# A three-stage attention and expert kernel: the hand-out of Strassen inputs and of the first pair's GpSimd sums, moved to later steps

## The chip, the cores and the metric

The kernel runs on one core of a Trainium2 chip. The metric is the device time of one execution in microseconds (us). Engines are named as the profile names them: PE (TensorE matmul; PEld its weight load), DVE (VectorE), ACT (ScalarE), POOL (GpSimd) and SP (SyncE, which here only issues DMAs).

## What is computed

Three stages follow each other (cut from the reference):

```
attn_out = attention(q, k, v)          # 4 x 8 heads, 576 positions, two masks
x = attn_out as 2304 tokens x 512
h = x @ w_in;  x = (h - tanh(h)) @ w_out              # 512 -> 2048 -> 512
xn = x / sqrt(mean(x*x) + 1e-6) * rms_g
y = (silu(xn @ w_gate) * (xn @ w_val)) @ w_out2       # 512 -> 1536 -> 512
```

## The kernel before

Every fp32 product is made of three matmuls on a high and a low half (`hi*hi + hi*lo + lo*hi`), so each operand needs a cast (high) and a subtraction (low) before PE can use it.

The attention and the first expert run until about 466 us. The second expert works on the first 256 tokens plainly and on the other 2048 by one level of Strassen's scheme (seven products in place of eight). The **plain part** is the loop over `f` at lines 1388 to 1399, 12 steps (`FB` = 12), one for each 128 columns of `w_gate` and `w_val`. A step prepares weights ahead (`st2.to`: load `raw`, ACT splits the bits at L184 and L186, DVE merges them into `ct` at L196, ACT casts the high half at L203, DVE subtracts the low half at L207), stores the merged weights to DRAM (`v`, L344, from ACT's queue) and the split ones (`w`, L363, from SP's), and issues the step's matmuls (`pe_gv`, into `ps_h`), then those of the step two before into the output sums (`pe_o`, into `ps_x`). `pe_gv` also issues the step's activation: SiLU (L949), product (L950), high and low half `p` (L952, L953).

Two generators are drawn from in the same loop:

- `pg` is `preps()`. When the loop begins seven items are left: `conv(m)` for m = 1, 2, 5, 6, 3, 7, 4. Each makes one Strassen input `xt` for tokens 256 to 1279: a subtraction `tr` (L1039, for m = 5, 6, 7 and 4), a cast (L1058, ACT) and a subtraction (L1059, DVE) on 128x1024 tiles.
- `decode.to(n)` runs the first n of a list. For the first **pair** (two 128-column blocks of the weights) these are eight: load the four stored tiles `v` into two `wa` tiles (L291), four sums or differences `ws` on POOL (L302) and the high and low halves `wo` of the results (L285, L286), for gate and then for val; one of the eight is empty. The tiles `tr`, `wa` and `ws` share a pool of four buffers.

After the loop comes `Stage.run` for the first pair: product 1 (`ps_pr` from `wt`), the last plain `pe_o`, then product 5 (`ps_pr` from `wo`), product 2 (`ps_q`), and 6, 3, 7, 4. Product 5 multiplies by the first `wo` of gate and then of val.

The order on the engines is made when the program is built: a scheduler with a model of its own sorts ACT, DVE and POOL by the place in the program and by priorities (`tc.high_priority`), while SP and, after the loop, PE keep the order of the program. A tile is written only when a buffer of its pool is free. DMAs of SP and ACT share eight completion counters in turn, and each DMA waits until the one that used its counter before has landed.

Of the kernel before, what the change touches and what calls it, by code (L numbers as in the profile page):

```python
# [34 lines left out]
def attn_moe_moe_kernel(  # L35
# [25 lines left out]
    B, _, NC, D = q_str.shape  # L61
    NT, DM = out.shape
    FA = w_in.shape[0]
    FB = w_gate.shape[0]
# [16 lines left out]
    def runs(s):  # L81

        r = []
        for i, (b, t) in enumerate(subs[s]):
            if r and r[-1][0] == b and r[-1][1] + r[-1][2] == t:
                r[-1][2] += 64
            else:
                r.append([b, t, 64, 64 * i])
        return r
# [36 lines left out]
    for s in range(len(subs)):  # L126
        if len(runs(s)) > 1 or s in LANES:
            _, t0, n, _ = runs(s)[0]
# [201 lines left out]
    decode = Decode()  # L330
# [606 lines left out]
    def pe_gv(j, f):  # L937
        r, n = [], R0
        bank = (bank_h, bank_m, bank_h, bank_m, bank_x, bank_x)[f % 6]("ps_h")
        for k, kd in enumerate(("gate", "val")):  # L940
            ps = bank[:, k * n:k * n + n]
            w, x = w2[kd, f].t, xn[j]
            seq = [(a, e, c) for c in range(4) for a, e in ((0, 0), (0, 1), (1, 0))]
            for i, (a, e, c) in enumerate(seq):
                mm(ps, w[:, a, c, :], x[:, e, c, :], i == 0, i == len(seq) - 1)
            r.append(ps)
        with tc.high_priority(400):
            s = pb.tile([128, n], F32, tag="s", name="s", bufs=3)
            nc.scalar.activation(out=s, in_=r[0], func=ACTF.Silu, scale=WS)  # L949
            nc.vector.scalar_tensor_tensor(out=s, in0=r[1], scalar=WS, in1=s, op0=ALU.mult, op1=ALU.mult)  # L950
            t = pb.tile([128, 2, n], F32R, tag="p", name="p", bufs=3)
            nc.scalar.copy(out=t[:, 0], in_=s)  # L952
            nc.vector.tensor_tensor(out=t[:, 1], in0=s, in1=t[:, 0].bitcast(F32), op=ALU.subtract)  # L953
        p_of[j, f] = t

    def pe_o(j, f):
        if f == 0:
            oacc[j] = [ps_x.tile([128, 512], F32, tag="x", name="ps_x") for _ in range(R0 // 128)]
        w, p = w2["out2", f].t.rearrange("p s c f -> p s (c f)"), p_of.pop((j, f))
        for t in range(R0 // 128):  # L960
            for i, (a, e) in enumerate(((0, 0), (1, 0), (0, 1))):
                mm(
                    oacc[j][t], p[:, e, t * 128:t * 128 + 128], w[:, a, :],
                    f == 0 and i == 0, f == FB - 1 and i == 2,
                )
# [422 lines left out]
    for f in range(FB):  # L1388
        if f == FB - 4:
            pairs[0].fetch((0, 1))  # L1390
        st2.to(max(3 * (f + 2), N1 + (len(w2_order) - N1) * (f + 1) // (FB - 2)))
        store.plain(st2.i - 1)
        store.to(st2.i - 6)
        pe_gv(0, f)
        for _ in range(3 if f < FB - 2 else 40):
            next(pg, None)
        decode.to(max(0, min(8, 8 * (f - 4) // 6)))
        if f > 1:
            pe_o(0, f - 2)
    pe_o(0, FB - 2)  # L1400
# [154 lines left out]
```

## Time and profile before

| | us |
|---|---|
| median of 3 runs | 888.45 |
| lowest, highest run | 885.4, 888.65 |
| profiled execution, its own time | 887.88 |
| its span | 886.1 |
| PE busy in the span | 866.5 |
| DVE, ACT, POOL busy | 629.8, 413.9, 250.6 |

The span is counted from the first instruction; about 1.8 us of the execution's own time lie outside it. In a timeline a row merges instructions of one kind that follow each other: start, duration, engine, line, tiles, count, and in brackets how long the engine stood idle before and what released it. `SPq` and `ACTq` rows are the queues at which DMAs are issued. The table by stretch gives for each engine the busy us and the number of instructions, then the clock granted to PE as a share of full speed, the busy share of the DMA engines and the rate.

### The profile page before, as it was taken

To read this page: it belongs to the slowest core of one execution; us is meant where nothing else is said; L and a number is where in the kernel's file an instruction comes from. 1 tells how busy PE (TensorE), PEld (TensorE's weight loads), DVE (VectorE), ACT (ScalarE), POOL (GpSimd) and SP (SyncE) were. 2 spreads that over 40 slices of the span, in tenths; PEclk is the share of its full clock that TensorE was granted. 3 is DMA by queue.
4 is the path that set the end of the run, shared out by engine and by line. 5 is a ranking of instruction groups with operands and counts; after the bars stand their busy time and mean duration, and the time that the engine had idled before them with its cause. 6 is when DMAs were issued, how large, how long until landed. Compare 5 with 4: busy or idle time off the path is not lost.

```text
span 886.1 us, 14047 instructions
## 1 busy us (share of the span) xinstructions
PE 866.5 (98%) x5091; PEld 722.7 (82%) x5091; DVE 629.8 (71%) x1290; ACT 413.9 (47%) x916; POOL 250.6 (28%) x309
## 2 busy tenths in 40 slices
PE   7999999999999999999999899999999999999998
PEld 4888888888998887888889877888788888888886
DVE  5999778888779887657778945569688553445544
ACT  6887633333543333878657644533325324322230
POOL 0000147695366853000000679846200000000000
PEclk8999999999999999999999999999999999999999
DMA  9965224311313000889977999765661288544002
GB/s 302 368 223 178 74 75 156 104 57 36 115 55 110 25 19 27 330 306 370 412 252 227 352 372 336 299 230 214 211 216 48 75 320 353 177 149 136 1 1 95
DMA packets 63717, 164.12 MB, mean 185 GB/s; under 512 B 10080, under 2 KB 21728, under 8 KB 63648
## 3 DMA queue, kind: packets, MB, share of 16 engines
q1 hardware_dynamic: 61088, 159.56, 51.1%
q10 hardware_dynamic: 2560, 3.67, 1.2%
q8 instruction: 40, 0.66, 0.3%
q14 instruction: 29, 0.24, 0.1%
HBM read 119.16 MB, written 44.04 MB: 184 GB/s over the span
## 4 chain that ended last, share of the span: by engine, by line
PE 58%; DVE 10%; POOL 7%; issue 2%; ACT 2%; DMA 1%; SPq 0%; ACTq 0%; DVEq 0%; POOLq 0%
PE ps_pr L150 20%; PE ps_o L150 14%; PE ps_h L150 10%; PE ps_x L150 9%; POOL pr L675 5%; DVE so L715 4%; PE ps_q L150 4%; POOL pr L708 1%; DVE tg L860 1%; DVE g L871 1%; DMA wt<-w 1%; DMA w<-w 1%; DVE s L1108 0%; DVE sm L451 0%; POOL ws L302 0%
## 5 line engine op out<-in xcount | busy, mean ns | idle before, releaser
L150 PE MATMUL ps_h<-xs,w 128*128 128x512 f32 (+1 forms) x984 | 214.6, 367 | 0.7 <-DVE tg L860 0.7
L150 PE MATMUL ps_x<-g,w 128*128 128x512 f32 (+1 forms) x984 | 214.2, 366 | 0.0
L150 PEld LDWEIGHTS ps_h<-xs,w 128*128 128x128 f32 x984 | 169.9, 190 | 30.5 <-DVE tg L860 1.3
L150 PEld LDWEIGHTS ps_x<-g,w 128*128 128x128 f32 x984 | 168.5, 189 | 30.4 <-ACT g L866 0.4
L150 PE MATMUL ps_pr<-xt,wt 128*128 128x512 f32 x576 | 137.6, 390 | 2.0 <-DVE s L1118 1.1
L150 PE MATMUL ps_o<-wt,p 128*128 128x512 f32 x576 | 136.0, 389 | 0.0
L150 PEld LDWEIGHTS ps_pr<-xt,wt 128*128 128x128 f32 x576 | 107.7, 188 | 26.2 <-DVE s L1118 2.0
L150 PEld LDWEIGHTS ps_o<-wt,p 128*128 128x128 f32 x576 | 108.1, 188 | 22.5
L675 POOL TENSOR_TENSOR pr<-sk,sq 128x256 f32<-128x256 f32 (+2 forms) x101 | 82.6, 852 | 133.0 <-DMA sq<-in_q_str_dram 107.3
L866 ACT CAST g<-tg 128x512 fp32r<-128x512 f32 (+1 forms) x82 | 46.5, 567 | 101.3 <-DVE tg L860 101.2
L1129 ACT COPY u<-ps_pr 128x512 f32<-128x512 f32 x72 | 41.9, 587 | 103.5 <-PE ps_pr L150 103.4
L708 POOL TENSOR_TENSOR pr<-sv,se 128x288 f32<-128x288 f32 (+12 forms) x104 | 69.7, 691 | 57.0 <-DVE so L715 19.8
L1181 DVE SCALAR_TENSOR_TENSOR osum<-ps_o,osum 128x512 f32<-128x512 f32 x80 | 54.8, 687 | 27.2 <-PE ps_o L150 26.6
L302 POOL TENSOR_TENSOR ws<-wa 128x256 f32<-128x256 f32 x24 | 24.6, 1044 | 170.4 <-DVE w L207 152.2
L715 DVE TENSOR_REDUCE so<-pr 128x16 f32<-128x272 f32 (+11 forms) x104 | 64.9, 653 | 9.0 <-POOL pr L708 8.6
L150 PE MATMUL ps_pr<-xt,wo 128*128 128x512 f32 x288 | 67.4, 389 | 0.0
L150 PEld LDWEIGHTS ps_pr<-xt,wo 128*128 128x128 f32 x288 | 54.1, 188 | 11.3
L871 DVE TENSOR_TENSOR g<-tg,g 128x512 fp32r<-128x512 f32 (+1 forms) x82 | 55.3, 676 | 10.6 <-ACT g L866 9.3
L860 DVE SCALAR_TENSOR_TENSOR tg<-ps_h,tg 128x512 f32<-128x512 f32 (+1 forms) x82 | 50.6, 618 | 15.9 <-ACT tg L855 15.6
L855 ACT ACTIVATE tg<-ps_h 128x512 f32<-128x512 f32 (+1 forms) x82 | 44.2, 540 | 34.8 <-PE ps_h L150 34.7
L196 DVE SCALAR_TENSOR_TENSOR ct<-ca,ct 128x512 uint32<-128x512 uint32 x68 | 48.0, 713 | 16.6 <-ACT ca L186 16.0
L680 DVE TENSOR_REDUCE sc<-pr 128x4 f32<-128x256 f32 (+2 forms) x101 | 43.7, 437 | 12.1 <-POOL pr L675 11.7
(121 smaller groups left out, 1045.7 us busy)
## 6 DMA issues: line engine op xcount, KB each, us to landing
wt<-w SPq DMA_DIRECT2D x84, 512.0 KB, 4.6
w<-w SPq DMA_DIRECT2D x36, 512.0 KB, 6.2
raw<-in_w_out_dram SPq DMA_DIRECT2D x28, 512.0 KB, 5.8
w<-wo SPq DMA_DIRECT2D x24, 512.0 KB, 7.4
raw<-in_w_in_dram SPq DMA_DIRECT2D x16, 512.0 KB, 8.6
raw<-in_w_gate_dram SPq DMA_DIRECT2D x12, 512.0 KB, 6.7
raw<-in_w_val_dram SPq DMA_DIRECT2D x12, 512.0 KB, 7.1
wa<-v SPq DMA_DIRECT2D x24, 256.0 KB, 4.7
```

The lines of the kernel that those rows point to most:

```text
L150: nc.tensor.matmul(out_, lhsT, rhs, start=start, stop=stop, skip_group_check=True)
L196: nc.vector.scalar_tensor_tensor(out=t, in0=self.a.bitcast(U32), scalar=3, in1=t, op0=ALU.logical_shift_left, op1=ALU.bitwise_or)
L675: nc.gpsimd.tensor_tensor(out=pr, in0=self.k[:, a:e, :], in1=self.q[:, c - c0:c - c0 + 1, :].to_broadcast([128, e - a, D]), op=ALU.mult,)
L680: pend.append(lambda: nc.vector.tensor_reduce(out=s[:, c - c0, a:e], in_=pr, axis=AX.X, op=ALU.add))
L708: nc.gpsimd.tensor_tensor(out=pr, in0=self.v[:, 0:c + 1, a:e], in1=self.e[:, c - c0, 0:c + 1].unsqueeze(2).to_broadcast([128, c + 1, e - a ...
L715: pend.append(lambda: nc.vector.tensor_reduce(out=o[:, c - g0, a:e], in_=pr.rearrange("l c d -> l d c"), axis=AX.X, op=ALU.add))
L855: nc.scalar.activation(out=t, in_=h_of[g, f, a], func=ACTF.Tanh, scale=WS)
L860: nc.vector.scalar_tensor_tensor(out=t, in0=h_of.pop((g, f, a)), scalar=WS, in1=t, op0=ALU.mult, op1=ALU.subtract)
L866: nc.scalar.copy(out=t[:, 0], in_=t_of[g, f, a])
L871: nc.vector.tensor_tensor(out=t[:, 1], in0=t_of.pop((g, f, a)), in1=t[:, 0].bitcast(F32), op=ALU.subtract)
L1129: nc.scalar.copy(out=u, in_=x[kd])
L1181: nc.vector.scalar_tensor_tensor(out=o, in0=ps, scalar=WS, in1=o, op0=ALU.mult, op1=ALU.add)
```

## The change

```
-        for _ in range(3 if f < FB - 2 else 40):
+        for _ in range((f >= 5) + (f == 5) if f < FB - 2 else 40):
             next(pg, None)
-        decode.to(max(0, min(8, 8 * (f - 4) // 6)))
+        decode.to(max(0, 8 * (f - 7) // 4))
```

Before, the seven inputs were handed out in steps f = 0 (three), 1 (three) and 2 (one). Now f = 5 hands out two, f = 6 to 9 one each, and f = 10 the last. Of the eight items for the first pair, f = 5 did the loads and f = 6 to 10 the rest; now f = 8 does the loads and gate's sums, f = 9 gate's halves, f = 10 val's sums, and f = 11 val's halves.

The order that results, first on DVE around the weights of the ninth step. Before (`w_5882` is the gate weight of that step, `xt_5706` the shared tile of inputs 3 and 7; the subtraction `tr_5821` for input 7 stands one row above the first):

```order
L1059 TENSOR_TENSOR xt_5706<-x2_5239,xt_5706 128x1024
L207 TENSOR_TENSOR w_5773<-ct_5721,w_5773 128x512
L196 SCALAR_TENSOR_TENSOR ct_5827<-ca_5829,ct_5827 128x512
L1059 TENSOR_TENSOR xt5_5703<-tr_5762,xt5_5703 128x1024
L950 SCALAR_TENSOR_TENSOR s_5973<-ps_h_5948,s_5973 128x256
L207 TENSOR_TENSOR w_5778<-ct_5768,w_5778 128x512
L196 SCALAR_TENSOR_TENSOR ct_5877<-ca_5879,ct_5877 128x512
L950 SCALAR_TENSOR_TENSOR s_6014<-ps_h_5989,s_6014 128x256
L1059 TENSOR_TENSOR xt6_5704<-tr_5815,xt6_5704 128x1024
L1059 TENSOR_TENSOR xt_5706<-tr_5821,xt_5706 128x1024
L950 SCALAR_TENSOR_TENSOR s_6077<-ps_h_6052,s_6077 128x256
L207 TENSOR_TENSOR w_5882<-ct_5827,w_5882 128x512
```

With the change the subtraction for input 7 and the low half that uses it no longer stand there; they stand at the end, woven into the last step's activation:

```order
L207 TENSOR_TENSOR w_6191<-ct_6130,w_6191 128x512
L1039 TENSOR_TENSOR tr_6227<-x2_5239 128x1024
L950 SCALAR_TENSOR_TENSOR s_6313<-ps_h_6288,s_6313 128x256
L1059 TENSOR_TENSOR xt_5706<-tr_6227,xt_5706 128x1024
L953 TENSOR_TENSOR p_6316<-s_6313,p_6316 128x256
```

The other six inputs stay within a few rows of where they were. On SP's queue, before (`raw_6147` is the last `w_val` block, `wt` the weights of product 1):

```order
L363 DMA w3_6_146<-w_5778 256x1x256
L291 DMA wa_6020<-v0_0_110 128x512
L291 DMA wa_6020<-v0_1_111 128x512
L291 DMA wa_6023<-v0_2_112 128x512
L291 DMA wa_6023<-v0_3_113 128x512
L175 DMA raw_6032<-in_w_val_dram 128x512
L166 DMA w_6039<-w5_7_173 128x1024
L363 DMA w4_0_153<-w_5882 128x1024
L363 DMA w4_1_154<-w_5887 128x1024
L175 DMA raw_6094<-in_w_gate_dram 128x512
L280 DMA wt_6143<-w0_0_101 128x1024
L280 DMA wt_6145<-w0_1_102 128x1024
```

With the change the four `wa` loads stand behind eleven more DMAs:

```order
L175 DMA raw_6070<-in_w_gate_dram 128x512
L280 DMA wt_6117<-w0_0_101 128x1024
L280 DMA wt_6119<-w0_1_102 128x1024
L175 DMA raw_6121<-in_w_val_dram 128x512
L166 DMA w_6128<-w5_8_174 128x1024
L363 DMA w4_6_159<-w_5921 256x1x256
L363 DMA w4_6_159<-w_5964 256x1x256
L291 DMA wa_6174<-v0_0_110 128x512
L291 DMA wa_6174<-v0_1_111 128x512
L291 DMA wa_6177<-v0_2_112 128x512
L291 DMA wa_6177<-v0_3_113 128x512
```

On POOL, with the change, from val's first sums on (`wo_6231` and `wo_6319` are gate's and val's weights of product 5):

```order
L302 TENSOR_TENSOR ws_6277<-wa_6177 128x256 x2
L286 TENSOR_TENSOR wo_6231<-ws_6180,wo_6231 128x512
L286 TENSOR_TENSOR wo_6234<-ws_6180,wo_6234 128x512
L302 TENSOR_TENSOR ws_6277<-ws_6277,wa_6177 128x256
L302 TENSOR_TENSOR ws_6277<-wa_6177,ws_6277 128x256
L285 CAST wo_6319<-ws_6277 128x512
L285 CAST wo_6322<-ws_6277 128x512
L286 TENSOR_TENSOR wo_6319<-ws_6277,wo_6319 128x512
```

Before, all eight sums stood ahead of all four casts; now gate's casts and low halves are woven with val's sums, as they are for the later pairs. PE's order after the loop is the same in both.

## Rows read from the trace of the kernel before

**Rows 1.** The page: shares of the chain that ended last, by engine.
```profile
PE 58%; DVE 10%; POOL 7%; issue 2%; ACT 2%; DMA 1%; SPq 0%; ACTq 0%; DVEq 0%; POOLq 0%
```

**Rows 2.** Table by stretch: us, busy by engine (instructions), PE clock, DMA share, GB/s.
```profile
480.00:490.00 10.00, 9.29 (x61) 8.16 (x60) 10.00 (x13) 9.90 (x18) 0.00 (x0) 1.00 0.87 293
...
510.00:520.00 10.00, 8.57 (x50) 7.17 (x48) 5.35 (x8) 3.98 (x8) 6.48 (x6) 1.00 1.00 379
```

**Rows 3.** The same table in stretches of 2 us around two stalls of PE.
```profile
492.00:494.00 2.00, 0.16 (x2) 0.10 (x1) 2.00 (x4) 0.41 (x1) 0.00 (x0) 1.00 0.99 301
494.00:496.00 2.00, 2.00 (x13) 2.00 (x14) 2.00 (x5) 1.51 (x4) 0.57 (x1) 0.69 1.09 367
496.00:498.00 2.00, 2.00 (x6) 1.61 (x6) 2.00 (x4) 1.75 (x4) 2.00 (x1) 0.50 0.94 252
498.00:500.00 2.00, 2.00 (x14) 1.76 (x14) 2.00 (x4) 1.29 (x3) 2.00 (x2) 0.96 0.91 338
...
518.00:520.00 2.00, 0.57 (x6) 0.37 (x4) 0.47 (x2) 0.79 (x2) 0.00 (x0) 1.00 0.90 303
```

**Rows 4.** Timeline of PE, 487 to 522: start, us, work, [idle before, releaser].
```profile
487.10 2.25 PE L150 MATMUL ps_h<-xn,w 128*128 128x256 f32 x14 [0.30 <-DVE w L207]
489.70 1.19 PE L150 MATMUL ps_x<-w,p 128*128 128x512 f32 x4 [0.36 <-ACT p L952]
...
493.90 2.26 PE L150 MATMUL ps_h<-xn,w 128*128 128x256 f32 x12 [1.84 <-DVE w L207]
...
516.95 1.60 PE L150 MATMUL ps_h<-xn,w 128*128 128x256 f32 x12
519.98 1.66 PE L150 MATMUL ps_x<-w,p 128*128 128x512 f32 x6 [1.43 <-ACT p L952]
521.47 2.91 PE L150 MATMUL ps_pr<-xt,wo 128*128 128x512 f32 x12
```

**Rows 5.** Timeline of DVE, 484 to 503.
```profile
484.09 1.22 DVE L1039 TENSOR_TENSOR tr<-x 128x1024 f32<-128x1024 f32 x1
...
490.57 2.35 DVE L1059 TENSOR_TENSOR xt<-tr,xt 128x1024 fp32r<-128x1024 f32 x2
...
493.17 0.68 DVE L207 TENSOR_TENSOR w<-ct,w 128x512 fp32r<-128x512 f32 x1
...
501.15 1.23 DVE L207 TENSOR_TENSOR w<-ct,w 128x512 fp32r<-128x512 f32 x1
```

**Rows 6.** Timeline of SP's queue: the `wa` loads and the load of `wt`.
```profile
490.31 2.94 SPq L291 DMA_DIRECT2D wa<-v  x4
...
503.62 0.79 SPq L280 DMA_DIRECT2D wt<-w  x2
```

**Rows 7.** DMA issues at 490.3, 494.5, 503.6 and 508.4: KB each, median us to landing.
```profile
wa<-v SPq DMA_DIRECT2D x4, 256.0 KB, 4.3
...
v<-ct ACTq DMA_DIRECT2D x1, 256.0 KB, 9.1
...
wt<-w SPq DMA_DIRECT2D x2, 512.0 KB, 6.5
...
w<-w SPq DMA_DIRECT2D x1, 512.0 KB, 8.9
```

**Rows 8.** Timeline of POOL: first and last work of the first and second pair.
```profile
495.43 4.71 POOL L302 TENSOR_TENSOR ws<-wa 128x256 f32<-128x256 f32 x2 [152.24 <-DVE w L207]
...
513.48 3.00 POOL L286 TENSOR_TENSOR wo<-ws,wo 128x512 fp32r<-128x512 f32 x2
521.98 1.44 POOL L302 TENSOR_TENSOR ws<-wa 128x256 f32<-128x256 f32 x2 [5.50 <-DMA wa<-v]
...
533.43 1.29 POOL L286 TENSOR_TENSOR wo<-ws,wo 128x512 fp32r<-128x512 f32 x1
```

**Rows 9.** Timeline of ACT: a cast of a Strassen input, an issue of `v`.
```profile
496.90 1.04 ACT L1058 CAST xt<-tr 128x1024 fp32r<-128x1024 f32 x1 [0.25 <-DVE tr L1039]
497.50 0.33 ACTq L344 DMA_DIRECT2D v<-ct  x1
```

## The prediction

> **What bounds the kernel now.** I read the chain that ended last first: 58% of it is PE, 10% DVE, 7% POOL [rows 1]. So time is won where PE waits, and what delays PE costs in full. The table by stretch then shows where the change lies: from 480 to 490 us DVE is busy all 10.00 us and ACT 9.90, with PE at 9.29; from 510 to 520 DVE has time (5.35), but the DMA engines are full (share 1.00) [rows 2]. The reader is to see two different limits, first DVE and ACT, then DMA and POOL.
>
> In PE's timeline the plain part has five stalls that matter here [rows 4]: 0.30 and 1.84 us for the low half of a weight (DVE, L207), 0.36 for `p`, and 1.43 for the last `p` at 519.98. The fifth shows only in the clock: after the stall of 1.84 the granted clock is 0.69, then 0.50, the lower of its two levels (1.2 in place of 2.4 GHz), and back near 1.00 from 498 [rows 3]. The first 12 matmuls took 2.26 us, where the same 12 take 1.60 at 516.95 [rows 4]. Half speed over most of 493.9 to 498.1 is a loss of about 4.2 x 0.5 = 2.1 us. After the 1.43 at 519.98 the six matmuls took 1.66, so that stall was not followed by it.
>
> Product 5 begins at 521.47 without a wait and, by its 12 matmuls, ends at 524.2 [rows 4]. Its weights were ready early: POOL worked on the first pair from 495.43 to 516.48 [rows 8], 5 us ahead.
>
> **The change part by part.**
>
> *Strassen inputs.* The number of instructions is the same. Though seven inputs are handed out later, the scheduler puts six of them where they were, since DVE reaches them only when the tokens are scaled. Only input 7 moves: a subtraction of 1.22 and a low half of 2.35/2 = 1.18 on DVE [rows 5], with a cast of 1.04 on ACT [rows 9]. DVE was full, so all that stands behind in its queue comes 2.4 us earlier. The weight that PE waited for until 493.85 (493.17 + 0.68 [rows 5]) then is there at about 491.5, the stall of 1.84 goes, that of 0.30 too (the subtraction stood ahead of that weight as well), and with them the 2.1 of the clock. For the wait for `p` I take 0.55 in place of 0.36, since more of DVE's weight work now stands ahead of it. Sum up to the end of the last plain `ps_h` at 518.55 (516.95 + 1.60 [rows 4]): -0.30 - 1.84 - 2.1 + 0.2 = -4.0, so **514.5**.
>
> *The end of the plain part.* Input 7's cast (1.04) now stands between the last SiLU and the cast of the last `p`, and its low half (1.18) ahead of `p`'s low half. Of the 2.2 some 1.2 can show, since the cast runs beside DVE's product. From the end of `ps_h` to product 5 it took 521.47 - 518.55 = 2.9; now 4.1. PE is ready for product 5 at **518.6**, 2.9 earlier than before. If POOL were done by then, the kernel would gain 2.9.
>
> *The loads for the first pair.* They leave SP at 490.31 to 493.25 [rows 6] and now stand behind eleven more DMAs. The last `w_val` block, four places ahead of the first `wa`, waits by its counter for the `v` of the tenth step, which was issued at 497.50 [rows 9] and now is at about 495.3. A `v` of this stretch took 9.1 to land [rows 7], the shortest DMA near it 4.3. I take the middle, 6.7: 502.0. That block and three more DMAs take SP some 0.5 each, and each half of gate's `wa` 0.7 (2.94/4 [rows 6]), so gate's second half leaves some 3 us later, at about **505**, with 502.6 and 507.4 as the ends. To landing it is between 4.3, what `wa` took at 490, and 8.9, a store issued at 508.38 [rows 7]. I take the nearest row in time, 6.5 for the two loads at 503.6 [rows 7]: POOL can begin at **511.5** (506.9 to 516.3).
>
> *POOL.* The work is the same, but it now has to be done just before its use. The second pair, in the same woven order, took from 521.98 until val's low half ended at 533.43 + 1.29 = 534.72: 12.7 us [rows 8]. The first took 495.43 to the middle of the last row, 514.98: 19.5, beside a full DVE and with one load still on its way. I take 12.7, because DVE at 511 to 524 is as it was beside the second pair and not as it was at 495. Gate's weights, about 7 us after the beginning, are there at 518.5, when PE comes for them. Val's low half is there at 511.5 + 12.7 = **524.2**. Two of val's six matmuls need the high half alone, four the low half, 0.9 us: product 5 ends at 525.1, against 524.2 before: **+0.9**. So the 4.0 won on DVE are all paid back at POOL, and PE stands still for some 4 us between gate's and val's half of product 5.
>
> *The clock after that stall.* 1.84 us of standing still was followed by a loss of 2.1 [rows 3, 4], 1.43 by none. Four us are past both, so I add **+2.1**. The Trainium skill ("TensorE: Matmul & The Clock Gate", What's actually happening) says the clock is halved after the engine idled and comes back only after sustained work; by that rule this stall brings the drop, and the drop at 494 agrees. Without the drop the sum would be +0.9.
>
> *What comes behind.* POOL's second pair begins about 3 us later and ends near 538; PE wanted it near 547, so that is covered by 9 us of slack. The two stores of product 5's weights and the loads behind them on SP move by no more than 3 us too. Freeing DVE and the DMA engines of 1 MB between 490 and 498 gives PE nothing more, since PE then runs without a wait until 518.55.
>
> **Sum:** 0.9 + 2.1 = +3.0 on the profiled execution's 887.88, which is 0.57 below the median of the runs. Against the median: 888.45 + 3.0 = **891.4**.
>
> **The rivals.**
>
> *POOL is on time (chance 0.21).* If `v` and `wa` land as the `wa` did at 490, in 4.3, POOL begins at 506.9 and val is ready at 519.6. Then the end of the plain part rules: 2.9 are gained, 885.5, and no drop follows. For it: those loads did take 4.3, and SP's stop until 503.62, at `wt`, goes away. Against it: the DMA engines are full [rows 2], and every other DMA near took 6.5 or more. A gain over 0.5% (4.4 us) would need savings behind product 5 as well: 0.05 of this.
>
> *The clock stays up (0.15).* POOL is late as forecast, but the 4 us are cut in two by the two matmuls on val's high half and the clock is not lowered: 889.4.
>
> *DVE holds up POOL, slower (0.22).* DVE subtractions with both inputs in SBUF took 0.68 while POOL was idle and 1.23 beside it [rows 5], and POOL's own first pair 19.5 in place of 12.7 [rows 8]. Now input 7's 2.4 us of just this kind and the last `p` fall on POOL's first sums. If POOL needs the mean of its two durations, 16.1, val is ready at 527.6, product 5 ends at 528.5, 4.3 later than before, and with the clock's 2.1 the kernel takes 894.9. At 19.5 it would be 898.3. It decides from 14.1 on: there the sum passes +4.4. Late loads (516.3 in place of 511.5) have the same effect, +4.8. The Trainium skill ("SBUF — State Buffer", Who interferes with whom) says that such a DVE instruction and a POOL one that reads SBUF exclude each other for their whole length; by that rule POOL loses up to each of these rows' length. The rows agree in direction; how much of it falls into 511 to 524 no row can say.
>
> *The inputs don't move as told (in all cases).* If the stalls at 487 to 494 stayed, because ACT, at 9.90 of 10, and not DVE set them, PE would reach product 5 at about 522.6 and wait less for POOL. The end is set by POOL either way, which itself hangs on these weights: about +3 to +5. I give it 0.07 within the range.
>
> **How the numbers follow.** Forecast (GpSimd late by some 4 us, clock lowered) 0.35, its own range 889 to 893.5; rivals 0.21, 0.15, 0.22, 0.07. A measurement of this kernel can tell about 0.5% from no change, so 884.0 to 892.9 is the same. Faster: 0.05. Slower: 0.18 of the 0.22 (POOL at 14.1 or more), 0.04 from the forecast's upper end and 0.03 of the last rival: 0.25. Same: 0.70. The range reaches from POOL on time (885.5) to DVE holding it up (894.9) with some room for a longer hold: **885.5 to 896.0**.
>
> **What the profile after would show.** The stalls of PE at 487 and 494 gone and the clock at 1.00 through 490 to 500. The `wa` loads leaving near 505, POOL's first sum near 511. An idle time of PE ahead of `ps_pr` from `wo` that POOL ends, of about 4 us in two parts, and a lower clock behind it. Wrong: no wait for POOL there (then the gain of 2.9 should show), a POOL row at 506 or before, a PE wait for `w` still at 494, or a second pair late at product 5 near 547.

## The result and the profile after

| | before | changed |
|---|---|---|
| median, us (runs) | 886.8 (10) | 891.52 (10) |
| lowest, highest | 884.77, 888.65 | 889.33, 893.38 |
| profiled execution, its span | 887.88, 886.1 | 892.58, 890.8 |

The ratio is 1.0051, with an interval of 1.0037 to 1.0066: slower by 4.5 us. The interval leaves out 1, so the loss is shown; it is small, at the 0.5% that the forecast took as the line between the same and slower. The forecast was 891.4. The sum is right, in part by luck; several of its terms are not.

The two traces don't start alike. Both have the same 24 matmuls ahead of the first wait of PE that differs, and these place one trace against the other. PE's timeline before:

```profile
481.91 3.04 PE L150 MATMUL ps_h<-xn,w 128*128 128x256 f32 x24
...
524.22 2.88 PE L150 MATMUL ps_q<-xt,wt 128*128 128x512 f32 x12
```

PE's timeline after, from the same 24 matmuls on:

```profile
482.64 3.04 PE L150 MATMUL ps_h<-xn,w 128*128 128x256 f32 x24
...
492.11 1.67 PE L150 MATMUL ps_x<-w,p 128*128 128x512 f32 x6 [0.77 <-DVE p L953]
...
509.10 1.20 PE L150 MATMUL ps_x<-w,p 128*128 128x512 f32 x4 [0.96 <-ACT p L952]
...
516.22 1.46 PE L150 MATMUL ps_h<-xn,w 128*128 128x256 f32 x10 [0.68 <-DVE w L207]
519.45 0.73 PE L150 MATMUL ps_x<-w,p 128*128 128x512 f32 x2 [1.77 <-ACT p L952]
521.52 2.08 PE L150 MATMUL ps_x<-w,p 128*128 128x512 f32 x4 [1.34 <-DVE p L953]
523.39 2.77 PE L150 MATMUL ps_pr<-xt,wo 128*128 128x512 f32 x6
526.62 0.98 PE L150 MATMUL ps_pr<-xt,wo 128*128 128x512 f32 x2 [0.47 <-POOL wo L285]
528.41 1.20 PE L150 MATMUL ps_pr<-xt,wo 128*128 128x512 f32 x4 [0.80 <-POOL wo L286]
529.45 2.89 PE L150 MATMUL ps_q<-xt,wt 128*128 128x512 f32 x12
```

So the trace after is late by 482.64 - 481.91 = 0.73 us before anything was moved; **aligned** times below have this taken off. The stalls of 0.30 and 1.84 [rows 4] are gone, only 0.77 is left near 492. But the last plain `ps_h` ends at 516.22 + 1.46 = 517.68, aligned 516.95: 1.6 us before the old 518.55, where 4.0 were forecast. From there to product 5 (the first `wo` row) it takes 523.39 - 517.68 = 5.7 us, and product 5 lasts until 529.45, 6.1 us in place of 2.75. Its end, where `ps_q` begins, is aligned at 528.72, **4.5 us later than before** (524.22). The spans differ by 4.7 - 0.73 = 4.0, so 0.5 comes back behind it: ahead of the second pair PE waits 1.09 us for DVE, where before it waited 0.67, 0.17 and 0.66.

The table by stretch after, in 10 and then in 2 us:

```profile
490.00:500.00 10.00, 9.23 (x59) 8.21 (x58) 10.00 (x18) 7.71 (x15) 0.00 (x0) 1.00 1.04 400
...
519.00:521.00 2.00, 0.73 (x2) 0.30 (x2) 1.88 (x2) 0.39 (x2) 2.00 (x2) 0.84 1.09 340
521.00:523.00 2.00, 1.48 (x4) 1.21 (x5) 0.46 (x1) 0.65 (x2) 2.00 (x3) 0.50 0.93 323
...
527.00:529.00 2.00, 1.20 (x5) 0.62 (x5) 0.00 (x0) 0.00 (x0) 2.00 (x3) 0.95 0.18 68
```

The clock stays at 1.00 where it fell before [rows 3] and falls in a new place: in the tail behind the last plain product, at 519 to 521, so before PE has met POOL at all. POOL's timeline, the first sum and val's last low half, and SP's queue with the `wa` loads:

```profile
514.03 1.59 POOL L302 TENSOR_TENSOR ws<-wa 128x256 f32<-128x256 f32 x2 [170.09 <-DMA wa<-v]
...
527.09 1.27 POOL L286 TENSOR_TENSOR wo<-ws,wo 128x512 fp32r<-128x512 f32 x1
```

```profile
505.42 3.45 SPq L291 DMA_DIRECT2D wa<-v  x4
```

POOL needs 528.36 - 514.03 = 14.3 us, and the last four matmuls of product 5 start 0.05 us after it: POOL sets product 5's end. ACT's timeline at the last weight and in the tail:

```profile
511.89 0.33 ACTq L344 DMA_DIRECT2D v<-ct  x1
512.26 0.78 ACT L184 ACTIVATE ct<-raw,colf 128x512 uint32<-128x512 uint16 x1 [2.19 <-DMA w<-w]
...
517.77 0.38 ACT L949 ACTIVATE s<-ps_h 128x256 f32<-128x256 f32 x1 [2.79 <-PE ps_h L150]
518.05 1.04 ACT L1058 CAST xt<-tr 128x1024 fp32r<-128x1024 f32 x1
518.99 0.41 ACT L952 CAST p<-s 128x256 fp32r<-128x256 f32 x1
```

ACT issues the store `v` of the last gate weight at 511.89 and only then takes up the last val weight, after 2.19 us of waiting that a DMA ended. DVE's timeline at the end:

```profile
516.08 1.75 DVE L1039 TENSOR_TENSOR tr<-x 128x1024 f32<-128x1024 f32 x1
...
519.12 1.48 DVE L1059 TENSOR_TENSOR xt<-tr,xt 128x1024 fp32r<-128x1024 f32 x1 [0.51 <-ACT xt L1058]
520.52 0.94 DVE L953 TENSOR_TENSOR p<-s,p 128x256 fp32r<-128x256 f32 x1
```

Input 7 stands in the tail as foreseen: ACT's cast of 1.04 between SiLU and the cast of `p`, DVE's low half ahead of `p`'s. Its DVE rows take 1.75 and 1.48 beside POOL, in place of 1.22 and 1.18 [rows 5].

### The profile page after: what moved, and what is told of

Read it like the earlier page. It is cut to its first block, busy times and chain, and to the rows that moved or that the text cites. A ratio compares the mean times of both kernels' runs of the same rounds, so it can differ in the third digit from the quotient of the medians.

```text
span 890.8 us, 14048 instructions
## 1 busy us (share of the span) xinstructions
PE 869.4 (98%) x5091; PEld 724.0 (81%) x5091; DVE 627.9 (70%) x1290; ACT 413.3 (46%) x916; POOL 245.3 (28%) x309
## 4 chain that ended last, share of the span: by engine, by line
PE 55%; DVE 12%; POOL 8%; DMA 3%; issue 3%; ACT 1%; ACTq 0%; SPq 0%; DVEq 0%; POOLq 0%
PE ps_pr L150 19%; PE ps_o L150 13%; PE ps_h L150 9%; PE ps_x L150 8%; POOL pr L675 5%; DVE so L715 4%; PE ps_q L150 3%; DMA w<-w 1%; POOL pr L708 1%; DMA raw<-in_w_gate_dram 1%; DVE tg L860 1%; DVE g L871 1%; DVE s L1108 1%; DVE osum L1181 0%; DVE sm L451 0%
## 5 line engine op out<-in xcount | busy, mean ns | idle before, releaser
L302 POOL TENSOR_TENSOR ws<-wa 128x256 f32<-128x256 f32 x24 | 21.5, 918 | 182.2 <-DMA wa<-v 170.1
L150 PE MATMUL ps_pr<-xt,wo 128*128 128x512 f32 x288 | 69.5, 396 | 1.3 <-POOL wo L286 0.8
```

The costliest lines, as they stand in the source:

```text
L150: nc.tensor.matmul(out_, lhsT, rhs, start=start, stop=stop, skip_group_check=True)
```

## The experiments

Two theories stood at first. **P**: POOL's late sums set the end. **T**: the end of the plain part does, by its late last weights and by input 7 in the tail. After four runs a third took their place. **G**: both stand as gates less than 1 us apart. Later **D** and **S** ask whether there is any place where input 7 and the sums cost nothing; the expectations define them. Diffs are against the changed kernel unless said otherwise.

All runs in one table. Columns: ratio to before with interval; the stall of PE near 494; the end of the last plain `ps_h`, then begin and end of product 5, against before, aligned by the 24 matmuls; the length of product 5; PE's waits for POOL in it.

| run | ratio | stall | plain | begin | end | length | POOL |
|---|---|---|---|---|---|---|---|
| changed | 1.0051 [1.0037, 1.0066] | 0.77 | -1.6 | +1.2 | +4.5 | 6.1 | 1.3 |
| e1 inputs only | 1.0083 [1.0065, 1.0102] | none | +5.5 | +5.4 | +5.4 | 2.7 | 0 |
| e2 sums only | 1.0065 [1.0047, 1.0083] | 1.83 | +0.5 | +0.7 | +4.6 | 6.7 | 3.0 |
| e3 sums earlier | 1.0020 [1.0003, 1.0037] | 0.78 | +0.3 | +1.7 | +2.9 | 4.0 | 0 |
| e4 fewer sums | 1.0046 [1.0029, 1.0063] | 0.76 | -1.4 | +2.0 | +2.7 | 3.5 | 0 |
| e5 input 7 early | 1.0055 [1.0038, 1.0072] | 2.48 | 0.0 | +0.5 | +4.6 | 6.8 | 2.3 |
| e6 both early | 1.0007 [0.9989, 1.0025] | 2.49 | +0.5 | +1.7 | +2.5 | 3.6 | 0 |
| e7 store on SP | 1.0074 [1.0050, 1.0098] | 0.77 | -3.0 | -0.5 | +4.9 | 8.2 | 2.9 |
| e8 all three | 1.0014 [0.9997, 1.0032] | 2.48 | +0.4 | +0.8 | +0.8 | 2.8 | 0 |
| e9 input 7 between | 0.9989 [0.9974, 1.0003] | 0.77 | -2.0 | -1.5 | -1.5 | 2.8 | 0 |
| e10 the same, store on SP | 0.9988 [0.9974, 1.0003] | 0.76 | -1.9 | -0.9 | -0.9 | 2.7 | 0 |

The ratio is taken from all executions of a session, the other columns from one profiled execution each. The profiled execution of before lost some 1.7 us to the lower clock behind its stall at 494 [rows 3]; against an execution without that loss, plain, begin and end would be that much higher. Where the profiled execution lies far from the median of its run, the text says so.

**e1: the new place of the inputs, the old one of the sums.**

```
-        decode.to(max(0, 8 * (f - 7) // 4))
+        decode.to(max(0, min(8, 8 * (f - 4) // 6)))
```

> The later hand-out of the Strassen inputs alone; the loads and sums for the first pair stay where they were in the kernel before. Theory P (the prediction's: the late sums on POOL cost everything that DVE gains): PE's stalls at 487 to 494 and the lower clock behind them go, 3 to 4 us, and POOL is early, so 2 to 4 us faster than before, ratio 0.996 to 0.998. Theory T (the end of the plain part sets when product 5 begins: late last weights, and input 7 woven into the last activation): input 7 stands some rows ahead of the end in this order, so some gain is left, but the last weights are as late as in the changed kernel: ratio 0.998 to 1.001.

Both missed: its ratio is the highest of all. POOL is no gate (no wait in product 5), yet product 5 begins 5.4 us late. DVE's timeline:

```profile
505.00 1.22 DVE L1039 TENSOR_TENSOR tr<-x,tr 128x1024 f32<-128x1024 f32 x1
...
508.00 2.35 DVE L1059 TENSOR_TENSOR xt<-tr,xt 128x1024 fp32r<-128x1024 f32 x2
510.27 1.22 DVE L1039 TENSOR_TENSOR tr<-x,tr 128x1024 f32<-128x1024 f32 x1
511.40 1.21 DVE L207 TENSOR_TENSOR w<-ct,w 128x512 fp32r<-128x512 f32 x1
```

Three subtractions `tr` (one more at 506.25) and three low halves `xt` (one more at 512.60) lie in one clump among the last weights, and PE waits 2.74 us for the `w` of 511.40. `tr`, `wa` and `ws` share four buffers, and with the loads at the sixth step `wa` has two of them before the inputs get theirs. That the buffers made the clump is read from the program's order; no run tests it. The two halves of the change are not independent.

**e2: the old place of the inputs, the new one of the sums.**

```
-        for _ in range((f >= 5) + (f == 5) if f < FB - 2 else 40):
+        for _ in range(3 if f < FB - 2 else 40):
```

> The later loads and sums alone; the seven Strassen inputs are handed out as in the kernel before, so input 7 is early on DVE and not woven into the last activation. Theory P: POOL begins near 513, val's low half is there near 527, product 5 ends 3 to 4 us later than before, and the clock is lowered: ratio 1.004 to 1.007. Theory T: product 5 begins as before or up to 1 us later, PE waits for POOL for 1 to 2 us: ratio 1.001 to 1.002.

P's figure was right, T's too low; the lower clock that P foresaw behind POOL did not come (the last four matmuls took 1.21). PE's timeline:

```profile
494.06 1.70 PE L150 MATMUL ps_h<-xn,w 128*128 128x256 f32 x12 [1.83 <-DVE w L207]
...
527.89 1.21 PE L150 MATMUL ps_pr<-xt,wo 128*128 128x512 f32 x4 [2.27 <-POOL wo L286]
```

With the inputs handed out as before, the late loads and sums alone cost 4.6 us at product 5's end. The first row is a second finding: the stall of 1.83 is before's 1.84 [rows 4], but the 12 matmuls behind it took 1.70 and not 2.26.

**e3 and e4: POOL in time.** e3 moves the sums earlier, e4 leaves six of eight out.

```
-        decode.to(max(0, 8 * (f - 7) // 4))
+        decode.to(max(0, 8 * (f - 6) // 5))
```

> The changed kernel with the loads in the eighth step (f = 7) in place of the ninth and the rest spread over f = 8 to 11. The wa loads stand six DMAs earlier on SP, so POOL should begin 3 to 5 us earlier than in the changed kernel. Theory P: PE's wait for POOL and the lowered clock go, 4 us less than the changed kernel, ratio to before 0.999 to 1.001. Theory T: only the visible wait of 1.3 us goes, ratio 1.003 to 1.004.

```
-            ):
+            )[:1 if self.p == 0 else 4]:
...
+            if self.p == 0:
+                self.part(2 + 2 * n + kd, self.t[kd][:, 0].unsqueeze(1).to_broadcast([128, 2, 256]))
+                return
```

> The changed kernel with six of the eight sums for the first pair left out (gate's and val's weights of the first pair are all made from the one sum that is left), with the same order on every other engine. POOL's chain to val's low half gets 5 to 6 us shorter; nothing else changes. Theory P: the wait of PE for POOL and the lowered clock behind it go: 3 to 4 us less than the changed kernel, ratio to before 1.001. Theory T: product 5 begins late anyway and at the lower clock, only the 0.47 and 0.80 us of waiting for POOL go: ratio 1.0035 to 1.004.

e3 fell between the theories, e4 near T. Neither waits for POOL, and product 5 still ends 2.9 and 2.7 us late. But e3 moved more than the sums. DVE's timeline with input 7's two rows, then PE's:

```profile
506.70 1.22 DVE L1039 TENSOR_TENSOR tr<-x 128x1024 f32<-128x1024 f32 x1
...
509.73 1.75 DVE L1059 TENSOR_TENSOR xt<-tr,xt 128x1024 fp32r<-128x1024 f32 x1
```

```profile
509.86 0.73 PE L150 MATMUL ps_x<-w,p 128*128 128x512 f32 x2 [1.37 <-DVE p L953]
...
522.05 4.13 PE L150 MATMUL ps_pr<-xt,wo 128*128 128x512 f32 x12
```

Input 7 left the tail and stands among the last weights, beside POOL. There it holds up `p` (1.37), the last plain `ps_h` ends at +0.3 and not at -1.6, and most of product 5 runs at half speed. So what remains in e3 is not input 7 in the tail but input 7 in another place where PE waits. Only e4 keeps the order of the changed kernel. PE's timeline in e4:

```profile
517.70 1.22 PE L150 MATMUL ps_x<-w,p 128*128 128x512 f32 x2 [1.77 <-ACT p L958]
520.31 2.08 PE L150 MATMUL ps_x<-w,p 128*128 128x512 f32 x4 [1.39 <-DVE p L959]
522.18 3.64 PE L150 MATMUL ps_pr<-xt,wo 128*128 128x512 f32 x12
```

The tail and the lower clock behind it are the same without any wait for POOL (L958 and L959 are L952 and L953 of the other kernels). So the lower clock comes behind the tail's stalls, and behind the gate of POOL a second one stands at +2.7. That value is from an execution of 887.06 us; e4's median is 889.74, and why most of its executions take longer no trace shows.

**e5: input 7 out of the tail, sums late.**

```
-        for _ in range((f >= 5) + (f == 5) if f < FB - 2 else 40):
+        for _ in range((f >= 5) + (5 <= f < 8) if f < FB - 2 else 40):
```

> The changed kernel with two inputs instead of one given out also on its seventh and eighth step: input 7 is then cast and subtracted beside the plain steps, ahead of the loads of the first pair's sums, and no longer in the tail behind the last weights. The sums keep their late place. Theory G (two gates stand less than 1 us apart, the tail behind the last weights and GpSimd's last half, and each alone sets product 5's end at +3.5 to +4.5 over before): the tail gets 1.5 to 3 us shorter, the wait for GpSimd's val half grows by as much, the ratio to before stays at 1.003 to 1.005. Theory T (the tail alone decides): 1.001 to 1.002.

As G has it, within the interval. PE's timeline:

```profile
494.25 1.65 PE L150 MATMUL ps_x<-w,p 128*128 128x512 f32 x6 [2.48 <-DVE p L953]
...
517.55 1.59 PE L150 MATMUL ps_h<-xn,w 128*128 128x256 f32 x12
...
522.60 2.67 PE L150 MATMUL ps_pr<-xt,wo 128*128 128x512 f32 x8
527.54 2.07 PE L150 MATMUL ps_pr<-xt,wo 128*128 128x512 f32 x4 [2.27 <-POOL wo L286]
```

The tail falls from 5.7 to 522.60 - 519.14 = 3.5 us, product 5 begins 0.7 earlier and ends where it did: POOL takes it all back, and half speed follows its wait (the last four matmuls 2.07). POOL's first sum in this run:

```profile
515.34 1.44 POOL L302 TENSOR_TENSOR ws<-wa 128x256 f32<-128x256 f32 x2 [171.60 <-DMA w<-w]
```

It begins 1.4 later (aligned) than in the changed kernel, and PE gets the last half at 527.54, 12.2 us after.
The stall near 494 is there again, at 2.48, because input 7 stands on DVE ahead of `p`.

**e6: input 7 early and the sums earlier** (the edits of e5 and e3).

> As the run with input 7 early, and the loads and sums of the first pair from the eighth step instead of the ninth, as in the run with the sums earlier. Theory G: both gates are open, product 5 follows the last plain products by 3 us and does not wait for GpSimd; what is left is the gain of the plain part (1.6 us), ratio 0.996 to 0.999. Theory D (GpSimd's sums take VectorE's SBUF bandwidth wherever they lie beside the last weights, so that there is nothing to be gained by moving them): the last weights come 1 to 2 us later than in the run with the sums late, ratio 1.000 to 1.002.

The ratio fell into D's range, but not for D's reason. PE's timeline:

```profile
494.28 2.40 PE L150 MATMUL ps_x<-w,p 128*128 128x512 f32 x6 [2.49 <-DVE p L953]
...
518.27 1.45 PE L150 MATMUL ps_h<-xn,w 128*128 128x256 f32 x10 [0.54 <-DVE w L207]
...
523.76 3.80 PE L150 MATMUL ps_pr<-xt,wo 128*128 128x512 f32 x12
```

Both gates are open. What this execution loses is lost near 494 (2.49 and a lower clock) and by a lower clock in product 5; it took 890.13 us, where e6's median is 887.06. The last weights hold PE up by 0.54 only, where D asked for 1 to 2.

**e7: the last store from SP's queue.**

```
-                    queue = nc.sync if cvt.name == "cvt" else nc.scalar
+                    queue = nc.sync if cvt.name == "cvt" or w.f == FB - 1 else nc.scalar
```

> The changed kernel with one edit: the stores of the merged weights of the last plain step are issued from SyncE's queue instead of ScalarE's, so that ScalarE does not stand at them. ScalarE takes the last val weight about 2 us earlier (at 510 instead of 512.3) and the last plain products end 1.5 to 2 us earlier. Theory G: the wait for GpSimd's val half takes the place, ratio 1.003 to 1.005. Theory T: 1.002 to 1.003. If ScalarE's wait was for the weight's own landing and not for its place in the queue, nothing moves: 1.005.

The mechanism is as told, the price was missed. PE's timeline, then SP's queue:

```profile
514.85 1.59 PE L150 MATMUL ps_h<-xn,w 128*128 128x256 f32 x12
...
526.28 1.06 PE L150 MATMUL ps_pr<-xt,wo 128*128 128x512 f32 x2 [2.06 <-POOL wo L285]
528.07 2.08 PE L150 MATMUL ps_pr<-xt,wo 128*128 128x512 f32 x4 [0.72 <-POOL wo L286]
529.94 4.50 PE L150 MATMUL ps_q<-xt,wt 128*128 128x512 f32 x12
```

```profile
509.53 0.32 SPq L344 DMA_DIRECT2D v<-ct  x1
...
511.16 2.08 SPq L291 DMA_DIRECT2D wa<-v  x4
```

The wait of 0.68 for the last weight is gone and the last plain product ends 1.35 us earlier, so ACT's place in its queue did cost that. But the store now waits on SP until 509.53, and the `wa` loads behind it leave at 511.16 in place of 505.42: the blocked queue only changed its owner. The loads then land in 4.1 us and not in 7.3, so POOL begins only 0.9 us later (aligned) and, with 13.0 in place of 14.3 us of work, has val's low half even 0.5 earlier. Product 5 begins 1.7 us earlier than in the changed kernel and ends 0.4 later, because its last four matmuls run at half speed (2.08 in place of 1.20). So does `ps_q` behind it (4.50 in place of 2.89): here the clock cost in full, behind 2.9 us of waiting for POOL.

**e8: e6 with the edit of e7.**

> Input 7 early, the sums from the eighth step, and the last step's merged weights stored from SyncE's queue. Theory G: another 1 to 2 us below the run with the first two, ratio 0.994 to 0.997, and no wait of TensorE over 0.8 us behind the last weight but the chain from the last SiLU to product 5. Theory D: no more than 0.5 us below that run, 0.999 to 1.002.

G's figure missed, D's held: with the sums' loads issued before it, the store on SP holds up no load of the first pair, and in the profiled execution (887.36 us, median 889.12) product 5 runs at full speed and ends at +0.8; but the stall near 494 remains. By the times it does not differ from e6.

**e9: input 7 between both places.** Two inputs at the sixth and seventh step, sums as in e3.

```
-        for _ in range((f >= 5) + (f == 5) if f < FB - 2 else 40):
+        for _ in range((f >= 5) + (5 <= f < 7) if f < FB - 2 else 40):
```

> Two inputs on the sixth and seventh step and one on each later step, the loads and sums of the first pair from the eighth step: input 7's subtraction and sum then stand on VectorE between the weights of the tenth and the eleventh step, neither ahead of the stall near 494 us (there in both runs with input 7 early, 2.48 us) nor in the tail. Theory S (input 7's 3.6 us on VectorE cost where VectorE is full, near 490 us, or where TensorE waits for the tail; from 500 to 512 us VectorE is idle half the time and they cost nothing): the stall near 494 is 0.8, the time from the last plain product to product 5 about 3 us, no wait for GpSimd; ratio to before 0.994 to 0.998. Theory D (whatever VectorE does beside GpSimd's sums takes longer, the last weights come as much later as the tail got shorter): 1.000 to 1.003.

S's mechanism holds; the ratio of 0.9989 lies just above its range, whose upper part the interval covers. DVE's timeline with input 7's two rows, then PE's:

```profile
499.40 1.22 DVE L1039 TENSOR_TENSOR tr<-x 128x1024 f32<-128x1024 f32 x1
...
502.75 1.23 DVE L1059 TENSOR_TENSOR xt<-tr,xt 128x1024 fp32r<-128x1024 f32 x1 [0.26 <-ACT xt L1058]
```

```profile
491.38 1.66 PE L150 MATMUL ps_x<-w,p 128*128 128x512 f32 x6 [0.77 <-DVE p L953]
...
519.99 2.91 PE L150 MATMUL ps_pr<-xt,wo 128*128 128x512 f32 x12
```

No stall near 494, no input in the tail, no wait for POOL, full speed in product 5, whose end is 1.5 us earlier than before. D is out: the last plain product ends at -2.0, without a wait for the last weights. This execution took 884.9 us. The medians are 886.72 against 887.73 of before in the same sessions. The interval reaches from 0.9974 to 1.0003: the loss of the change is gone, but that this version beats the kernel before is not shown.

**e10: e9 with the edit of e7.**

> As the run with input 7 between, and the merged weights of the last plain step stored from SyncE's queue. If ScalarE still stands at a store in the run with input 7 between, the last val weight comes up to 2 us earlier here and the ratio to before is 0.001 to 0.002 lower than there; if SyncE's later transfers (the weights of the first pair, the weight stores) pay for it, as in the run with that edit alone, it is 0.001 to 0.002 higher.

Neither happened (0.9988): in e9 the last weight was not held up any more, so there was nothing to win on ACT.

## Why the prediction was right, and where it was not

*The stalls of the plain part and the clock there.* Right in the place: 1.84 and 0.30 are gone, and the clock is at 1.00 from 490 to 500. e5, e6 and e8, where input 7 goes back to DVE's full stretch, have the stall again. "For the wait for `p` I take 0.55": it was 0.77. The 2.1 for the clock took half speed for 4.2 us; by the clocks of [rows 3] the loss is 2 x (0.31 + 0.50 + 0.04) = 1.7. Nor is it there in every execution: e2 has the stall and not the drop.

*"Sum up to the end of the last plain `ps_h`: -4.0".* Wrong, it was -1.6. The step that failed is "PE then runs without a wait until 518.55". Two new waits follow, 0.96 and 0.68, and after a plain part that runs earlier the weights are what is late. With the clock at 1.7 the waits add up: -0.30 - 1.84 - 1.7 + 0.41 + 0.96 + 0.68 = -1.8, near the -1.6 (0.41 is 0.77 less the old 0.36). The last one hung on ACT, which stood at issuing a store for 2.19 us; e7 shows that this was worth 1.35 us at the last plain product. The late loads seem to bring that block: in e2 and e5, where they leave at 507, ACT stands 5.76 and 4.57 us at the same store, in e3, e6 and e9, where they leave at 496 to 498, 1.1 at most; which earlier DMA the store waits for is not shown. The forecast asked how the stores delay SP's loads and not what stands behind them on ACT.

*"Of the 2.2 some 1.2 can show".* Wrong, the tail became 5.7 in place of 2.9, so 2.8 showed. e5 and e9, without input 7 in it, have 3.5 and, from the end of the last plain product at 514.99 + 1.59, 3.4 us. So some 2.2 of the 2.8 go with the input, as much as its cast and low half were to take: ACT's cast stood in the way of `p`'s, DVE's rows were longer beside POOL, and the four `ps_x` matmuls took 2.08 us at the lower clock. The other 0.6 is there without it; in e5 and e9 `p`'s low half on DVE takes 0.96 and 0.92 us beside POOL, before it took 0.43.

*The loads and POOL's begin.* Right for the loads: they leave from 505.42 on, aligned 504.7, gate's second half right behind the first, where "about 505" was forecast. To landing they took longer, by this answer on the DMAs issued from 505 to 509:

```profile
wa<-v SPq DMA_DIRECT2D x4, 256.0 KB, 7.3
```

I had taken 6.5. POOL began at 514.03, aligned 513.3, for 511.5, inside the ends given.

*"I take 12.7" for POOL.* Mis-sized: it took 14.3. Without input 7's subtractions beside it (e5) PE got its last half 12.2 us after POOL's first row (515.34 to 527.54). The Trainium skill ("SBUF — State Buffer", Who interferes with whom) says that a DVE instruction with two SBUF inputs contends with a GpSimd one that reads SBUF. The rows agree on both sides, 1.75 for 1.22 on DVE and 14.3 for 12.2 on POOL. e7, with input 7 in the tail too, shows 13.0: there the subtraction of input 7 is over (514.62) before POOL begins (515.03), and POOL's second and third row take 0.72 and 0.73 us; in the changed kernel, beside it, 1.18 and 1.59. Val's low half was ready at aligned 527.6, not 524.2. That is the value that the rival "DVE holds up POOL" gave, reached half by a later begin: the agreement to 0.1 is luck.

*"PE stands still for some 4 us".* Wrong: 1.3 us. PE came to product 5 at aligned 522.7, not 518.6, and then ran its first matmuls at half speed; both passed in time that it would have waited.

*"I add +2.1" for the clock.* The step that failed most. The clock did fall, but in the tail's stalls of 1.77 and 1.34, ahead of POOL's wait, as e4 shows without that wait. Half speed ahead of a gate costs nothing: the clock is back at 0.95 in 527 to 529 and the matmuls behind the gate run at full speed. The drop behind POOL's wait that was forecast does exist: e5 and e7 have it after waits of 2.27 and 2.06 us, e2 after one of 2.27 has not. So the end at POOL was +4.5 and not +0.9, and the clock on top was 0 and not +2.1, as the rival "The clock stays up" had it, though for another reason; with 0.5 back behind, +4.0 stands against the +3.0 forecast. Errors of opposite sign brought the sum near. By the medians the change cost 4.7 and not 3.0; the base of the forecast, 888.45, the median of three runs, lies 1.65 above that of all ten, and this hid the difference. That 891.4 lies 0.1 from the measured 891.52 is luck.

*POOL as the gate.* Right and shown: in e5 and e7 product 5 begins earlier and doesn't end earlier, and e2 pays 4.6 us for the late loads and sums alone. Not foreseen was the second gate: with POOL in time the tail holds the end at +2.7 (e4). Only e9 and e10 open both without closing the old one near 494. That the second pair is covered was right: near 546 PE waits for DVE only.

## What to carry to other kernels

Work that is moved off a full stretch has to be put where its engine is idle and nobody waits: input 7 cost 1.7 us of stall near 494 (2.48 in place of 0.77), some 2.2 in the tail and 2.3 among the last weights (e3's last plain product against e9's), and nothing that shows at 499 to 504. A transfer "just in time" has two prices, its own lateness and what queues behind its issue. And when two delays meet at one gate, take the later of them and not the sum; a lower clock counts only for what runs behind the gate.

## What was not expected of the hardware

The same stall does not always bring the same clock. The stall of 1.84 of before was followed by 0.50 [rows 3] and 2.26 us for 12 matmuls; e2's of 1.83 by this row of the table by stretch and 1.70 us:

```profile
494.00:496.00 2.00, 1.95 (x14) 1.91 (x15) 2.00 (x5) 1.36 (x3) 0.00 (x0) 1.00 1.00 404
```

e5's 2.48 was followed by six matmuls in 1.65, e6's 2.49 by six in 2.40, though PE's rows from the 24 matmuls up to that stall are the same in both within 0.03 us. The Trainium skill ("TensorE: Matmul & The Clock Gate", What's actually happening) ties the lower clock to idleness before. The traces agree in direction, but the length of one stall did not decide it here. A term for the clock is therefore a chance, not a sum. Two drops like the 1.7 at 494 would make the spread of some 4 us between runs of one kernel; of 28 runs of before the one of 884.66 us had a mean granted clock of 0.996, the one of 891.56 us of 0.988.
